# A scan and a bilinear feed-forward network on one core: the hand-written order of all tasks replaced by another, and the zero matmuls in float32

## The chip, the core and the metric

The kernel runs on one core of a Trainium2 chip. The core has a matrix engine (TensorE: PE for its matmuls, PEld for its weight loads), VectorE (DVE), ScalarE (ACT), GpSimd (POOL) and SyncE (SP, which here issues nearly all DMAs). Each engine works off its own list of instructions in order and waits on semaphores for the others. The metric is the device time of one execution in microseconds (us); lower is better.

## What is computed

The inputs are x (4 batches, 8 heads, 768 steps, 32 wide), decays a, and B and C (16 wide). A state per head is carried through time, and its output goes into a feed-forward network with four weight matrices that arrive in float64:

```python
for c in range(nc):                       # pieces of the sequence
    L = np.exp(cum[:, :, :, None] - cum[:, :, None, :]) * causal
    M = np.einsum('bhin,bhjn->bhij', Cc, Bc) * L
    y[:, :, sl] = M @ xc + (Cc @ state) * np.exp(cum)[..., None]
    state = decay_full * state + (Bc * decay_from_j).T @ xc
...
x = y.transpose(0, 2, 1, 3).reshape(3072, 256)
return ((x @ w1) * (x @ w2) @ w3) @ w_out
```

## The kernel before, in words

Every piece of work is a named task, and the string `PLAN` lists all of them in one order. A word `name:engine@banks` says which task comes next, on which engine (V is DVE, S is ACT, G is POOL, nothing is PE or a DMA on SP) and which PSUM banks or slots it gets. The loop at the end walks through the words and records each task; `tc.keep_in_program_order` keeps that order on every engine. So the list alone sets what stands behind what.

The sequence is cut into 16 chunks of 48 steps. For chunk c:
- `cN.X`, `cN.B`, `cN.N` load its inputs (tiles xe, bc, bn), `cN.K` loads decay sums for c of 2 and more. For chunks 0 and 1, `Y0`, `Y1` (DVE) build what `D0`, `D1` (PE) multiply instead; `a.clip`, `a.ln`, `a.scan`, `a.hi`, `a.lo`, `a.save` make the sums that later chunks load as `K`.
- `D0`, `D1` put exponents into a bank, `E0`, `E1` (ACT) take the exponential into tile r, `W0`, `W1` scale B into r, `CB` (PE, four banks) makes C times B, and `M0`, `M1` (DVE) multiply the halves into r.
- `MX` (PE, two banks) multiplies r with xe. `T` (DVE) transposes the state out, eight `Z` copies carry it into the next chunk's xe, and `hi`, `lo` (or `y`) bring the output into xa and xb, split in two float32r parts.

A product in the network is three float32r matmuls (high times high, high times low, low times high). Weights come in as float64 words: `.D` loads one into staging (tile early), then `.A` (ACT), `.L`, `.S` (DVE), `.H`, `.P` make the high and low parts. `wN` are the columns of w1 and w2, `oN` those of w_out, `vHK` those of w3; `vHK.M` (PE) multiplies w3 with w_out, and `e..` moves that into wo.

The 3072 rows are cut into seven slices. For slices 0 to 2, `lS.F.m` (PE) makes the two products, `.a` (ACT) copies one out of PSUM, `.g` (DVE) multiplies it with the other, `.h` and `.l` split the result. Slices 3 and 4, and 5 and 6, go in pairs through `pP.J` (sums of inputs), `zJ` (sums of weights) and seven products `sP.F.1` to `.7`, with `p`, `q`, `r`, `y`, `d`, `g`, `k` between. `dS.F` (PE) multiplies with wo, `dS.yT` copies out and `dS.xT` stores.

A word such as `+8@7` stands for eight matmuls of zeros into bank 7: their result is not used. There are 18, of bfloat16, 512 columns wide (helper `mm`, L151; memset L244). Their tile `zero` is 128 x 512 bfloat16.

The `ring` helper deals out staging slots (four), magnitude slots (five) and slots for w3 (four) in turn. `W` is always on GpSimd (`bw`), `hi` on ACT (`high`) and `.a` on ACT.

Of the kernel before, what the change touches and what calls it, by code (L numbers as in the profile page):

```python
# [30 lines left out]
c1.lo:V w2.S:V w1.A:S w1.L:V w2.H:S w2.P:V c2.D1@2 j.c:S c2.E0:S c1.Z5:S w1.S:V w7.L:V l0.0.m@3,4 w7.A:S w1.H:S w7.S:V l0.2.m@5,0 w1.P:V l0.2.a:S
w6.D w6.A:S c1.Z3:S w7.H:S c1.Z0:S l0.1.m@1,6 w6.L:V l0.2.g:V c3.N w6.S:V w7.P:V w4.D l0.0.a:S c2.B c2.N l0.7.m@7,5 w4.A:S l0.1.a:S c1.Z2:G c2.E1:S
w3.D c3.K c3.B w6.H:V w4.L:V c2.CB@0,1,2,3 w6.P:G l0.0.g:V c1.Z1:G c1.Z6:G c2.W1:G c2.W0:G l0.7.a:S c1.Z4:S w4.S:V l0.1.g:V w5.D c3.X l0.7.g:V
c2.M1:V c2.M0:V w4.H:S w3.A:S c4.B o0.D l0.6.m@4,7 c1.Z7:S w4.P:G w3.L:V w3.S:V w3.H:V w5.L:V c2.MX@5,6 c3.D1@3 c3.D0@2 c2.T:V c3.E1:S c2.hi:S
# [789 lines left out]
```

## Time and profile before

| | us |
|---|---|
| median of 3 runs | 264.28 (263.45 to 265.96) |
| the profiled execution | 263.44 |
| its span, first to last instruction | 261.6 |
| PE busy in it | 254.0 |
| DVE busy in it | 196.8 |

The span is what the trace covers; 1.84 us of the profiled execution's own time lies around it. Busy time is the union of an engine's instructions. Matmuls overlap and their ends are modelled, so a busy PE may still wait inside: the starts of successive matmuls tell more than the busy share. The granted clock of TensorE stands in a row as a share of 2.4 GHz.

### The profile page before, as it was taken

The numbers are of one execution on the slowest core, as the hardware profiler recorded it, in microseconds if no ns is written. First come the engines' busy times: TensorE is split into PE (matmuls) and PEld (weight loads), VectorE is DVE, ScalarE is ACT, GpSimd is POOL, SyncE is SP. The second block draws the span as 40 slices with busy tenths as digits, with TensorE's granted clock in tenths as the row PEclk, the third lists the DMA queues.
The fourth block names the chain that finished last, engine by engine and source line by source line (L and its number), as shares of the span: only waits on it lengthen the run. The fifth ranks groups of instructions, "written<-read, shape, count | busy, mean of one in ns | idle before, by whom it ended". The sixth has DMA issues, their size and how long they took to land.

```text
span 261.6 us, 7416 instructions
## 1 busy us (share of the span) xinstructions
PE 254.0 (97%) x2972; PEld 226.2 (86%) x2972; DVE 196.8 (75%) x354; ACT 141.4 (54%) x308; POOL 121.3 (46%) x160
## 2 busy tenths in 40 slices
...
GB/s 195 323 298 306 231 296 215 279 256 205 272 249 303 247 11 49 196 102 49 147 60 206 65 95 63 83 50 44 4 3 0 0 83 1 0 3 80 3 0 120
DMA packets 21754, 33.93 MB, mean 130 GB/s; under 512 B 3672, under 2 KB 13528, under 8 KB 21720
## 3 DMA queue, kind: packets, MB, share of 16 engines
...
HBM read 30.02 MB, written 3.44 MB: 128 GB/s over the span
## 4 chain that ended last, share of the span: by engine, by line
PE 85%; DMA 5%; DVE 4%; ACT 3%; issue 1%; SPq 0%; DVEq 0%
PE ps L151 85%; DMA xe<-in_x_dram 2%; DMA bc<-in_c_dram 2%; ACT fr L163 1%; DVE gs L157 1%; DMA gs<-in_Bt_dram 1%; DVE early L480 1%; DVE fr L157 0%; DVE early L160 0%; SPq L154 0%; ACT g L163 0%; ACT r L166 0%; DVE z L402 0%; ACT early L166 0%; ACT wo L163 0%
## 5 line engine op out<-in xcount | busy, mean ns | idle before, releaser
L151 PE MATMUL ps<-wo,fr 128*128 128x256 f32 x576 | 71.4, 281 | 0.0
L151 PEld LDWEIGHTS ps<-wo,fr 128*128 128x128 f32 x576 | 69.4, 189 | 1.2
L157 DVE TENSOR_TENSOR gs<-gs,ps 128x512 f32<-128x512 f32 (+1 forms) x73 | 43.6, 623 | 15.9 <-PE ps L151 10.4
L151 PE MATMUL ps<-xa,wh 128*128 128x384 f32 (+1 forms) x192 | 54.9, 366 | 0.2 <-DVE xa L157 0.2
L163 ACT COPY gs<-ps 128x512 f32<-128x512 f32 (+2 forms) x53 | 25.3, 492 | 47.6 <-PE ps L151 41.9
L151 PEld LDWEIGHTS ps<-xa,wh 128*128 128x128 f32 x192 | 34.6, 188 | 4.1 <-DVE xa L157 0.4
L151 PE MATMUL ps<-op,tw 128*128 128x512 f32 (+1 forms) x144 | 35.1, 366 | 0.0
L151 PE MATMUL ps<-xa,wl 128*128 128x384 f32 (+1 forms) x96 | 34.9, 363 | 0.0
L157 POOL TENSOR_TENSOR r<-bn,r 128x128 f32<-128x128 f32 x32 | 16.0, 507 | 35.5 <-ACT xe L163 13.6
L151 PEld LDWEIGHTS ps<-op,tw 128*128 128x128 f32 x144 | 25.8, 188 | 3.1 <-DVE gs L157 0.3
L157 POOL TENSOR_TENSOR fr<-gs,fr 128x512 fp32r<-128x512 f32 (+1 forms) x21 | 25.6, 1227 | 6.0 <-DVE fr L163 2.9
L151 PE MATMUL ps<-fr 128*128 128x256 f32 x192 | 25.4, 286 | 0.2 <-DVE fr L157 0.2
L151 PEld LDWEIGHTS ps<-fr 128*128 128x128 f32 x192 | 24.0, 191 | 1.2 <-DVE fr L157 0.4
L163 POOL COPY xe<-z 16x128 f32<-16x128 f32 x40 | 15.8, 394 | 14.4 <-issue 5.1
L157 DVE TENSOR_TENSOR r<-ps,r 128x384 f32<-128x384 f32 x32 | 17.2, 550 | 5.6 <-PE ps L151 4.8
L163 ACT COPY xe<-z 16x128 f32<-16x128 f32 x65 | 19.2, 296 | 1.6 <-DMA xe<-in_x_dram 0.3
L151 PEld LDWEIGHTS ps<-xa,wl 128*128 128x128 f32 x96 | 18.0, 188 | 2.0
L163 POOL CAST fr<-gs 128x384 fp32r<-128x384 f32 (+1 forms) x10 | 6.0, 601 | 28.5 <-PE ps L151 20.1
L166 ACT ACTIVATE early<-early 128x512 f32<-128x512 f32 x23 | 15.5, 675 | 6.1 <-DMA early<-in_w3t_dram 2.8
L480 DVE SCALAR_TENSOR_TENSOR early<-early 128x512 uint32<-128x512 uint32 x23 | 17.5, 760 | 1.4 <-ACT early L166 0.8
L163 ACT CAST fr<-gs 128x512 fp32r<-128x512 f32 (+1 forms) x23 | 13.8, 602 | 8.5 <-PE ps L151 8.4
L151 PE MATMUL ps<-op,wh 128*128 128x512 f32 (+1 forms) x64 | 18.2, 365 | 0.0
...
## 6 DMA issues: line engine op xcount, KB each, us to landing
...
bc<-in_Ct_dram SPq DMA_DIRECT2D x14, 320.0 KB, 4.6
xe<-in_x_dram SPq DMA_DIRECT2D x16, 256.0 KB, 4.1
early<-in_w_dram SPq DMA_DIRECT2D x16, 256.0 KB, 4.6
...
out_dram<-gs SPq DMA_DIRECT2D x22, 128.0 KB, 2.1
...
bn<-in_Bn_dram SPq DMA_DIRECT2D x14, 128.0 KB, 3.1
```

What stands on the lines that cost most here:

```text
L151: pin(nc.tensor.matmul(*args, **kw))
L157: pin((nc.gpsimd if e == "G" else nc.vector).tensor_tensor(*args))
L163: pin(nc.scalar.copy(*args) if e == "S" else (nc.gpsimd if e == "G" else nc.vector).tensor_copy(*args))
L166: pin(nc.scalar.activation(*args, **kw))
L480: pin(nc.vector.scalar_tensor_tensor(m, m, 3, v["wl"].bitcast(U32), ALU.logical_shift_left, ALU.bitwise_or))
```

## The change

The list of tasks is another one from the first word to the last: the tasks are the same (but for the zeros), with another order, other engines for 227 of them, and other banks and slots. Words in the list now also choose the staging and magnitude slot, the slot for w3, and the engine of `W`, `hi` and `.a`, so `ring` is gone. The matmuls of zeros are 6 (four at the start, two before `c1.MX`), and their operand is the first 512 columns of the tile fr, read as float32.

```diff
 PLAN = """
-t.D k.zero:V k.act:S +8@7 k.D1:D a.D c0.X t.clip:V c0.B c0.N w0.D t.ln:S k.R0:S k.keep:G k.L:V c0.Y0:V +1@7 c0.D0@0 a.clip:V a.ln:S c1.X k.D2:D c1.N
+k.zero:V k.act:S k.keep:G t.D k.D1 a.D w2.D@0 c1.N c0.N w0.D@1 a.clip:V c0.B t.clip:V k.L:V t.ln:S c0.X k.R0:S c1.Y0:V k.D2 c0.Y1:V a.ln:S +4@2
...
-    zero = sb([P, 512], BF16, "zero")
+    zero = FR[:, 0:512].bitcast(F32)
...
-        def bw(hf):
+        def bw(e, hf):
             gs = slice(hf * HG, (hf + 1) * HG)
-            tt("G", R[:, gs, 0:N], bp[:, gs, :], R[:, gs, TE - 1:TE].broadcast_to([P, HG, N]), ALU.mult)
+            tt(e, R[:, gs, 0:N], bp[:, gs, :], R[:, gs, TE - 1:TE].broadcast_to([P, HG, N]), ALU.mult)
...
-        def high(*at):
-            copy("S", place(0, *at), py(*at[1:]))
+        def high(e, *at):
+            copy(e, place(0, *at), py(*at[1:]))
...
-            v["st"] = ST[ring("st", NST)]
+            v["st"] = ST[b[0]]
...
-            v["mag"] = MAG[ring("mag", NMAG)]
+            v["mag"] = MAG[b[0]]
...
-            v["hi"], v["lo"] = hi(), lo()
+            v["hi"], v["lo"] = hi(b), lo()
...
-            slot["t"] = VR[:, ring("vr", 4)]
+            slot["t"] = VR[:, b[0]]
...
-            gate[sl, ft] = G5[k // 3][:, k % 3] if k < 15 else FREE[8][:, :384] if k == 15 else FREE[ft]
-            copy("S", gate[sl, ft], v[0])
+            gate[sl, ft] = G5[k // 3][:, k % 3] if k < 15 else FREE[b[0]][:, :BL[sl]]
+            copy(e, gate[sl, ft], v[0])
```

What the list does is seen in the instructions of each engine. On SP, the first eleven loads of before are these (la, gs and the array a are for the decays; early is staging for w0; xe, bc, bn belong to chunks 0 and 1 by their number):

```order
L154 DMA la<-in_Bt_dram 128x256
L154 DMA gs<-in_Bt_dram 128x352
L154 DMA gs<-in_a_dram 128x192
L154 DMA xe_82<-in_x_dram 128x512
L154 DMA bc_87<-in_c_dram 128x640
L154 DMA bn_84<-in_b_dram 128x256
L154 DMA early<-in_w_dram 128x2x256 x2
L154 DMA xe_83<-in_x_dram 128x512
L154 DMA gs<-in_Bt_dram 128x144
L154 DMA mask<-in_Bt_dram 128x48
L154 DMA bn_85<-in_b_dram 128x256
```

and of the change, where tile numbers are one lower from ld on:

```order
L154 DMA la<-in_Bt_dram 128x256
L154 DMA gs<-in_Bt_dram 128x352
L154 DMA gs<-in_a_dram 128x192
L154 DMA early<-in_w_dram 128x2x256 x2
L154 DMA bn_84<-in_b_dram 128x256
L154 DMA bn_83<-in_b_dram 128x256
L154 DMA early<-in_w_dram 128x2x256 x2
L154 DMA bc_86<-in_c_dram 128x640
L154 DMA xe_81<-in_x_dram 128x512
L154 DMA gs<-in_Bt_dram 128x144
L154 DMA mask<-in_Bt_dram 128x48
L154 DMA bc_87<-in_c_dram 128x640
```

Two whole weight loads, w2 and w0, now stand ahead of chunk 0's bc and xe, and chunk 1's bc and xe follow at once.

On PE, these are the last zeros ahead of `c0.D1` of before and then the tasks `c0.D1`, `c0.CB`, `c1.D0`, `c0.MX`, `c1.D1`, `c1.CB` (rd and gs are the two matmuls of a `D`, bc is `CB`, r with xe is `MX`):

```order
L151 MATMUL ps<-zero 128x512
L151 MATMUL ps<-rd,ld 128x384
L151 MATMUL ps<-gs 128x384
L151 MATMUL ps<-bc_87 64x96 x16
L151 MATMUL ps<-rd,ld 128x384
L151 MATMUL ps<-gs 128x384
L151 MATMUL ps<-r_89,xe_82 32x64 x32
L151 MATMUL ps<-rd,ld 128x384
L151 MATMUL ps<-gs 128x384
L151 MATMUL ps<-bc_88 64x96 x16
```

and the first rows of the change, where fr stands for the zeros and the tasks are `c1.D0`, `c0.D1`, `c0.D0`, `c0.CB`, `c1.D1`, `c0.MX`, `c1.CB`:

```order
L151 MATMUL ps<-fr 128x512 x4
L151 MATMUL ps<-rd,ld 128x384
L151 MATMUL ps<-gs 128x384
L151 MATMUL ps<-rd,ld 128x384
L151 MATMUL ps<-gs 128x384
L151 MATMUL ps<-rd,ld 128x384
L151 MATMUL ps<-gs 128x384
L151 MATMUL ps<-bc_86 64x96 x16
L151 MATMUL ps<-rd,ld 128x384
L151 MATMUL ps<-gs 128x384
L151 MATMUL ps<-r_88,xe_81 32x64 x32
L151 MATMUL ps<-bc_87 64x96 x16
```

Three `D` tasks now stand in a row ahead of `c0.CB`, and none is left between `c0.MX` and `c1.CB`.

On DVE, behind chunk 3's first `M` (r1 from ps) before, up to `c3.lo` (xb from ps), which frees chunk 3's banks:

```order
L157 TENSOR_TENSOR r1_90<-ps_66,r1_90 128x8x48
L480 SCALAR_TENSOR_TENSOR early_94<-early_94 128x512
L157 TENSOR_TENSOR r1_90<-ps_66,r1_90 128x8x48
L163 CAST wh_96<-early_94 128x512
L157 TENSOR_TENSOR wl_97<-early_94,wh_96 128x512
L402 STREAM_TRANSPOSE z_91<-ps_66 128x256
L157 TENSOR_TENSOR g1_69<-g1_69,ps_66 128x384 x2
L160 TENSOR_SCALAR early_94<-early_94 128x512
L157 TENSOR_TENSOR xb_93<-ps_66,xb_93 128x2x192
```

and of the change, from the first `M` of chunk 3 to the same `c3.lo`:

```order
L157 TENSOR_TENSOR r1_89<-ps_66,r1_89 128x8x48
L157 TENSOR_TENSOR g1_69<-g1_69,ps_66 128x384
L157 TENSOR_TENSOR r1_89<-ps_66,r1_89 128x8x48
L160 TENSOR_SCALAR early_93<-early_93 128x512 x2
L157 TENSOR_TENSOR wl_96<-early_93,wh_95 128x512
L474 SCALAR_TENSOR_TENSOR early_93<-early_93 128x512 x2
L160 TENSOR_SCALAR early_93<-early_93 128x512
L396 STREAM_TRANSPOSE z_90<-ps_66 128x256
L157 TENSOR_TENSOR xb_92<-ps_66,xb_92 128x2x192
```

Between the second `M` of chunk 3 and `c3.lo`, before has w5's cast and low part, the transpose, two `.g` and one `.L`; the change has w5's low part, the transpose and five steps of the weights v10, v11, o0 and v13. In the change `c4.CB`, second on PE behind `c3.MX`, writes banks 2 and 3, which `c3.lo` reads; before it takes the same banks, with `l0.5.m` and `l1.5.m` ahead of it.

## Rows read from the trace of the kernel before

**Rows 1.** The head of the page: the span, and each engine's busy time, share of the span and instructions.

```profile
span 261.6 us, 7416 instructions
...
PE 254.0 (97%) x2972; PEld 226.2 (86%) x2972; DVE 196.8 (75%) x354; ACT 141.4 (54%) x308; POOL 121.3 (46%) x160
```

**Rows 2.** The timeline of PE and its weight loads: start us, length us, engine, line, operation, tiles, shapes, count, and in brackets idle time ahead and what ended it. The first nine rows are of the start up to 17.22 us and the tenth is where the stream of `l0.0.m` begins for good; the last two are where `l0.5.m` starts and where it is followed by `l1.5.m`.

```profile
1.19 3.73 PE L151 MATMUL ps<-zero 128*128 128x512 bf16 x9 [1.19 <-DVE zero L244]
...
1.59 0.15 PEld L151 LDWEIGHTS <-zero 128*128 128x128 bf16 x1 [0.28 <-issue]
...
2.02 0.15 PEld L151 LDWEIGHTS <-zero 128*128 128x128 bf16 x1 [0.28 <-issue]
...
4.84 0.44 PE L151 MATMUL ps<-rd,ld 48*128 48x384 f32 x1
...
5.21 0.91 PE L151 MATMUL ps<-gs 128*128 128x384 f32 x2
...
5.96 0.81 PE L151 MATMUL ps<-zero 128*128 128x512 bf16 x3
...
7.92 0.59 PE L151 MATMUL ps<-bc 32*64 32x96 f32 x32
...
9.64 0.89 PE L151 MATMUL ps<-r,xe 64*32 64x64 f32 x64
...
12.06 0.59 PE L151 MATMUL ps<-bc 32*64 32x96 f32 x32 [0.31 <-DMA bc<-in_c_dram]
...
17.22 0.45 PE L151 MATMUL ps<-xa,wh 128*128 128x384 f32 x1 [0.15 <-DVE xa L157]
...
36.20 0.52 PE L151 MATMUL ps<-xa,wh 128*128 128x384 f32 x2
...
38.32 0.51 PE L151 MATMUL ps<-xb,wh 128*128 128x384 f32 x2
```

**Rows 3.** Three stretches: busy time of PE, PEld, DVE, ACT and POOL with their instructions, then granted clock, DMA share, GB/s.

```profile
0.00:6.00 6.00, 4.82 (x13) 1.81 (x14) 2.43 (x8) 3.25 (x5) 0.57 (x6) 1.00 0.64 187
6.00:10.00 4.00, 4.00 (x77) 1.88 (x76) 2.59 (x7) 1.88 (x4) 0.82 (x2) 1.00 1.03 332
17.20:38.40 21.20, 21.06 (x292) 19.52 (x293) 18.80 (x37) 15.72 (x36) 8.57 (x15) 1.00 0.85 284
```

**Rows 4.** DMA issues: tiles, engine, count, KB each, and where it is known the median us from issue to landing.

```profile
la<-in_Bt_dram SPq DMA_DIRECT2D x1, 128.0 KB
...
gs<-in_Bt_dram SPq DMA_DIRECT2D x1, 176.0 KB
...
gs<-in_a_dram SPq DMA_DIRECT2D x1, 96.0 KB
...
early<-in_w_dram SPq DMA_DIRECT2D x16, 256.0 KB, 4.6
...
bn<-in_b_dram SPq DMA_DIRECT2D x2, 128.0 KB, 4.4
...
bc<-in_c_dram SPq DMA_DIRECT2D x2, 320.0 KB, 4.5
...
xe<-in_x_dram SPq DMA_DIRECT2D x16, 256.0 KB, 4.1
```

**Rows 5.** The timeline of the start on DVE, POOL and ACT (columns as in rows 2): the memset of zeros, the first `W`, chunk 0's `M0` and `M1`, `c1.hi`, `c1.lo`.

```profile
0.86 0.27 DVE L244 MEMSET zero<- 128x256 uint32 x1 [0.86 <-PEq L805]
...
7.57 0.41 POOL L157 TENSOR_TENSOR r<-bn,r 128x128 f32<-128x128 f32 x1 [6.42 <-DMA bn<-in_b_dram]
...
8.61 1.02 DVE L157 TENSOR_TENSOR r<-ps,r 128x384 f32<-128x384 f32 x2 [1.40 <-PE ps L151]
...
16.09 0.48 ACT L163 CAST xa<-ps 128x384 fp32r<-128x384 f32 x1 [1.70 <-DVE z L402]
...
16.61 0.56 DVE L157 TENSOR_TENSOR xa<-ps,xa 128x384 fp32r<-128x384 f32 x1 [0.55 <-ACT xa L163]
```

**Rows 6.** DVE from 17.18 to 38.5 us, groups of one line and shape: count, busy us, mean ns of one, idle us ahead. In order: `.S`, `.g`, `.L`, `.P`, `M`, `T`.

```profile
L480 DVE SCALAR_TENSOR_TENSOR early<-early 128x512 uint32<-128x512 uint32 x7 | 5.5, 781 | 0.2
L157 DVE TENSOR_TENSOR g<-g,ps 128x384 f32<-128x384 f32 x7 | 3.6, 540 | 0.0
L160 DVE TENSOR_SCALAR early<-early 128x512 uint32<-128x512 uint32 x7 | 3.5, 495 | 0.0
L157 DVE TENSOR_TENSOR wl<-early,wh 128x512 fp32r<-128x512 f32 x4 | 2.8, 689 | 0.4 <-ACT wh L163 0.3
L157 DVE TENSOR_TENSOR r<-ps,r 128x384 f32<-128x384 f32 x4 | 2.1, 553 | 0.7 <-POOL r L157 0.6
L402 DVE STREAM_TRANSPOSE z<-ps 128x256 f32<-128x256 f32 x2 | 0.9, 446 | 0.5 <-PE ps L151 0.5
```

**Rows 7.** The timeline of PE's weight loads at three waits: ahead of `c5.MX`, in `v02.M`, ahead of `c8.MX`.

```profile
56.59 0.19 PEld L151 LDWEIGHTS ps<-r,xe 64*32 64x32 f32 x10 [0.64 <-ACT fr L163]
...
79.18 1.25 PEld L151 LDWEIGHTS ps<-fr 128*128 128x128 f32 x10 [0.45 <-DVE fr L157]
...
105.44 0.72 PEld L151 LDWEIGHTS ps<-r,xe 64*32 64x32 f32 x64 [0.93 <-ACT fr L163]
```

**Rows 8.** The timeline of DVE: one `z0.B`, which runs while POOL works.

```profile
97.65 2.33 DVE L157 TENSOR_TENSOR gs<-wh,wl 128x1024 f32<-128x1024 f32 x1
```

**Rows 9.** The group of all three `zJ.B` on DVE over the whole span: count, busy us, mean ns.

```profile
L157 DVE TENSOR_TENSOR gs<-wh,wl 128x1024 f32<-128x1024 f32 x3 | 4.9, 1631 | 0.0
```

More of the change, by code (lines that the diff above doesn't have):

```diff
@@ L31 @@
[L31 to L34, printed above, removed]
@@ new lines @@
+o0.H:S v10.P:G c3.T:V v12.D@3 c4.E1:S c3.lo:V v00.D@1 l0.3.g:V c4.CB@0,1,2,3 l0.5.a:S c4.W0:G c4.W1:V v11.A:S@4 l1.7.m@6,7 c4.M0:V c9.F1:G c7.N
+v13.A:S@2 c4.M1:V c5.B v11.S:V c6.N c3.Z1:G c3.Z3:V c8.K c9.F0:G c5.D1@0 l0.5.g:V c5.D0@1 l1.7.a:S@8 l1.5.m@2,3 c5.E0:S v12.L:V c3.Z4:G c5.X c3.Z0:S
+c3.Z6:G c6.B c3.Z5:S o1.D@0 v00.L:V c6.K l1.1.m@4,1 v13.S:V l1.5.a:S v11.H:S@1 l1.5.g:V c9.G1:V c3.Z7:S v02.D@2 v00.A:S@0 v11.P:G l1.4.m@6,5
+l1.1.a:S c3.Z2:S l1.1.g:V c5.W0:G c5.E1:S o0.P:V c5.W1:G l1.7.g:V c8.F1:G c4.MX@0,1 l1.4.a:S v12.A:S@3 l1.4.g:V c5.CB@6,7,3,4 c8.F0:G c4.hi:S c4.T:V
```

144 lines of the change are left out of this document (70 added, 74 removed).

## Prediction

> **What bounds the kernel now.** I read the page first: PE is busy for 254.0 of 261.6 us [rows 1], so the change can give only what PE still waits, and what lies ahead of its dense stream and behind it. Then the timeline of PE [rows 2]: what matters is when successive tasks start. Until 17.22 us the small products of chunks 0 and 1 and the zeros run; from 17.22, when `c1.lo` has ended, PE hardly stops. Then the stretches [rows 3]: DMA moves 332 GB/s from 6 to 10 us, so early on it is loads that are waited for; and from 17.2 to 38.4 DVE is busy for 18.80 of 21.20 us, so it is nearly a second bound there. Last the places where PE's weight loads stood still in the stream [rows 7]: 0.64, 0.45 and 0.93 us. A better order can win about these, and no more.
>
> The sum is made against the profiled execution, 263.44 us. The median of the three runs stands 0.84 us above it.
>
> **The zeros.** Before, weight loads of zeros start 0.43 us apart (1.59, 2.02) [rows 2]: 512 columns in 0.43 us are 1.2 GHz, the lower level. Three zeros at 5.96 take 0.81 us together, which is more columns in a us than the lower level has, so the clock is up by then. The nearest row for float32 is the second matmul of a `D`: 384 columns as two passes, from 5.21 to 5.96, so 0.75 us; 512 columns take 1.0 us at that clock, and at half of it 2.0 us as an upper end. The memset [rows 5] is twice as large, so the first zero starts not at 1.19 but about 0.27 later, at 1.46. If the clock is up by 4.84, as before, 3.4 us hold 1.7 zeros, and the other 2.3 end at 7.15. Three `D` follow, 1.12 us each (4.84 to 5.96): 10.5. If all four zeros run at the lower level they end at 9.5, and the `D` tasks at 12.8.
>
> **The loads.** How long a load takes is checked with chunk 0's bn: with it 1,104 KB have been issued (la 128, gs 176, a 96, xe 256, bc 320, bn 128 [rows 4]), or 1,130 kB. 187 GB/s move 1,122 kB by 6 us [rows 3], so its last byte moves at 6.0, and POOL, which waits for it, starts at 7.57 [rows 5]: 1.5 us more. In the change, chunk 0's bc is the last of 2,000 KB (la, gs, a, two halves of w2, two bn, two halves of w0, bc): 2,048 kB move by 8.8 us at 332 GB/s, and it lands at 10.3. Its xe is 256 KB later, at 11.1, and chunk 1's bc, 576 KB later, at 12.1. So `c0.CB` starts at about 10.5 instead of 7.92. The zeros and three `D` just fill the time until the load is there.
>
> **From there to the stream.** Before, `c0.CB` at 7.92 was followed by both `M` (8.61, 1.02 us [rows 5]) and `c0.MX` at 9.64 [rows 2], 1.72 us on. So `c0.MX` starts at 12.2 now and `c1.CB` 0.8 us behind it, at 13.0; before it started at 12.06, when its load was there. `CB` takes 0.5 us, the two zeros 2.0 us: 15.5. The `T` and both `M` that `c1.MX` needs end at about 15.2, so the zeros cost 0.3 us. `c1.MX` 0.8 us, a handover of 0.1, `c1.hi` 0.48 and `c1.lo` 0.56 [rows 5] (`c1.T` now stands behind them, which saves 0.45) give 17.5. **Start: +0.3 us**; at the fast end, with zeros that hide and loads 0.5 us earlier, -0.4; with all zeros at the lower level +2.3.
>
> **c2.D0 and c2.D1** stood ahead of 17.22, in PE's wait. Now they stand behind `l0.0.m`, because `a.lo` and so `a.save` come later on DVE and SP. A float32r product of 384 columns takes 0.18 us in `l0.5.m` (twelve from 36.20 to 38.32) and 0.37 us as the first matmul of a `D` (4.84 to 5.21) [rows 2], so two take 0.36 to 0.74; I take **+0.4**, near the former, since later loads overlap.
>
> **DVE in the first stretch.** From 17.22 to 38.32 PE does eight `l0` products, two `CB`, two `MX`, four `D` [rows 2]: 21.1 us. In the change the same work and two more `D`, 21.5 us, lies between the end of `c1.lo` and `c4.CB`, which must wait for `c3.lo` to free its banks. In the same stretch DVE's list has 41 instructions: 8 `.S` at 0.781, 9 `.L` at 0.495, 5 `.P` at 0.689, 6 `.g` and a copy like it at 0.540, 4 `M` at 0.553, 3 `T` at 0.446 [rows 6], two `lo` at 0.56 [rows 5], and three small ones, taken as 0.3 each. That is 6.25 + 4.46 + 3.45 + 3.78 + 2.21 + 1.34 + 1.12 + 0.9 = 23.5 us, where before had 18.80 in 21.2 us. DVE has done less ahead of 17.22 and takes on the first w3 and w_out weights earlier. So `c4.CB` could be 2.0 us late. Some of the 0.781 is stretch from other engines: a `.P`, also with two inputs and 512 columns, takes 0.689, and with that `.S` would save 0.7. I take **+1.3**; 0 if DVE finds that much slack, 3.0 with 1 us of waits for ACT's casts. Behind it are `l1.7.m`, which waits for `l0.3.g` just behind `c3.lo`, and the rest of PE's list.
>
> What a busy POOL does to DVE is seen in one pair of rows [rows 8, 9]: one `z0.B` took 2.33 us, while the three have 1.631 as mean, so the other two 1.28; a factor of 1.8. The change gives POOL `.H` of w7, w4, w3 and w5 and two `.P` in this stretch. The Trainium skill, GPSIMD Engine Reference, Specifications, says that GpSimd shares its SBUF interfaces with VectorE and contends with DVE instructions that have two SBUF inputs (or run in a two-port mode). By that rule `.S` and `.P` are all open to it, and the sum would come to the slower rival's 267.6. The rows' means speak for little of it, and I follow the means.
>
> **The waits that go.** Ahead of `c5.MX` (0.64) PE waited for a carry that stood behind `c5.M0` on DVE; in the new list chunk 4's carries come before that `MX` with `l1.2.g` between. In `v02.M` (0.45) it waited for `v02.P`, which stood right ahead of it in the list and now stands five PE tasks earlier. **-1.0** for both, 0 at worst. The third (0.93) stays: `c9.CB` and `c8.MX` share two banks and stand next to each other in both lists.
>
> **Sum:** 263.44 + 0.3 + 0.4 + 1.3 - 1.0 = 264.4. The rest is costed at nothing: the products are the same, and behind the last matmul there are three copies on the same two engines and three stores, as before.
>
> **Rivals.**
> - Faster. DVE keeps up (+0) as it starts the weights' steps in PE's small waits, the start is even or 0.4 early, and all waits go, the third among them (-2.0): 263.44 - 0.4 + 0.4 - 2.0 = 261.4, and with one half of that 262.4. For it: before, DVE had 2.4 us free in the same stretch. Against it: the sum of 23.5.
> - Slower, by POOL alone (the rule above): the 13 `.S` and `.P` of the stretch, 9.7 us, are stretched by POOL's casts. By a third each is +3.2 on top of 1.3: 267.6. Decides from 2.5 us of stretch (266.9). For it: the stretched row [rows 8]. Against it: the `.S` of before ran beside 8.57 us of POOL work [rows 3] and took 0.781 all the same.
> - The zeros don't save anything, but hold PE: all four at the lower level, start +2.3: 266.4. Against it: the clock was up by 5.96 before, and PE runs as densely now.
>
> **How the numbers follow.** My sum has 0.45 (263.2 to 265.6), the faster case 0.29 (261.0 to 263.2), the slower one 0.18 (266 to 268), the zeros 0.08. The range of 8 in 10 leaves out the end of the faster case and that of the slower: 261.3 to 267.3. About 1% is what a measurement of this kernel can tell from no change; around the median of before that is 261.6 and 266.9. Below lies half of the faster case, with noise 0.17; above lie three quarters of the slower one, and some of the zeros: 0.18; within is 0.65.
>
> **What would show it.** Right: `c0.CB` at 10 to 11 us waiting for bc or just behind the `D`; the second matmul of `l0.0.m` at 17.2 to 17.9; PE waiting 1 to 2 us for DVE at `c4.CB` or `l1.7.m`; no wait in `v02.M`, and one of 0.9 us at `c8.MX`. Wrong: a stream that starts before 16.7 or after 18.5; `.S` above 0.95 us in the first stretch; no wait of PE around 38 to 40 us; or new waits of over 1 us in the stretch of the `sP.F` products, which I have not costed as DVE has more room there.

## The result, and the profile after

| | before | change |
|---|---|---|
| median, four runs each | 264.78 us (263.45 to 265.96) | 267.43 us (266.59 to 268.16) |
| ratio, 95% interval | | 1.0118 (1.0078 to 1.0158) |
| the profiled execution | 263.44 | 267.43 |
| start of the second matmul of `l0.0.m` | 17.22 | 18.42 |
| start of `v10.M` | 58.17 | 61.37 |
| start of the last PE task, `d6.7` | 256.25 | 260.48 |

The change is slower by 1.2%. Two later sets of six runs of it gave 1.0126 (1.0083 to 1.0169) and 1.0145 (1.0106 to 1.0183). The last rows cut the time in three. Between the second matmul of `l0.0.m` and `v10.M` both lists do the same PE work, but for `c2.D0` and `c2.D1`, which are 0.35 us: 40.96 us before and 42.94 now. From `v10.M` to `d6.7` the work is the same too: 198.08 and 199.12. So the start lost 1.2 us, the middle 2.0, the rest 1.0. This cut is of one profiled execution of each: that of before is the fastest of its four, that of the change lies at its median, so they differ by 4.0 us where the medians differ by 2.65.

The page of the change, span and busy times [rows 1]:

```profile
span 265.6 us, 7397 instructions
...
PE 257.4 (97%) x2966; PEld 227.0 (85%) x2966; DVE 203.1 (76%) x362; ACT 133.5 (50%) x288; POOL 131.4 (49%) x172
```

PE is busier by 3.4 us with the same products: its zeros take 8.3 us (6.33 and 1.98 below) where those of before took 6.0, which is 2.3 of it, and a matmul that waits inside counts as busy. The start of PE's timeline [rows 2] tells more (fr are the zeros):

```profile
1.45 6.33 PE L151 MATMUL ps<-fr 128*128 128x512 f32 x8 [1.45 <-DVE fr L238]
7.71 0.44 PE L151 MATMUL ps<-rd,ld 48*128 48x384 f32 x1
...
8.92 0.44 PE L151 MATMUL ps<-rd,ld 48*128 48x384 f32 x1
...
11.34 0.59 PE L151 MATMUL ps<-bc 32*64 32x96 f32 x32
...
13.19 0.86 PE L151 MATMUL ps<-r,xe 64*32 64x64 f32 x64
13.97 0.59 PE L151 MATMUL ps<-bc 32*64 32x96 f32 x32
14.49 1.98 PE L151 MATMUL ps<-fr 128*128 128x512 f32 x4
16.40 0.86 PE L151 MATMUL ps<-r,xe 64*32 64x64 f32 x64
...
17.83 1.03 PE L151 MATMUL ps<-xa,wh 128*128 128x384 f32 x2
19.02 0.33 PE L151 MATMUL ps<-xa,wl 128*128 128x384 f32 x1 [0.16 <-issue]
```

And the weight loads of the zeros, in PEld's timeline:

```profile
5.03 0.34 PEld L151 LDWEIGHTS ps<-fr 128*128 128x128 f32 x1 [0.52 <-issue]
5.88 0.34 PEld L151 LDWEIGHTS ps<-fr 128*128 128x128 f32 x1 [0.52 <-issue]
6.74 0.22 PEld L151 LDWEIGHTS ps<-fr 128*128 128x128 f32 x1 [0.52 <-issue]
...
15.03 0.19 PEld L151 LDWEIGHTS ps<-fr 128*128 128x128 f32 x1 [0.24 <-issue]
15.45 0.19 PEld L151 LDWEIGHTS ps<-fr 128*128 128x128 f32 x1 [0.24 <-issue]
```

A zero is recorded as two matmuls of 512 columns (x8 for the four), and one of these takes 0.85 us until 6.74 and 0.42 us at 15: of the first four zeros three ran at the lower level (1.45 to 6.74), and the fourth took 0.97 us. The three `D` tasks are 1.21 us apart, not 1.12.

The places in the stream where PE stood [rows 7], in its timeline:

```profile
40.37 0.59 PE L151 MATMUL ps<-bc 32*64 32x96 f32 x32 [0.33 <-DMA bc<-in_Ct_dram]
...
43.67 0.58 PE L151 MATMUL ps<-rd,ld 96*128 96x384 f32 x2 [0.42 <-DMA ld<-cq]
...
108.15 0.86 PE L151 MATMUL ps<-r,xe 64*32 64x64 f32 x64 [0.72 <-DVE r L157]
...
185.21 1.65 PE L151 MATMUL ps<-op,tw 128*128 128x512 f32 x6 [0.53 <-DVE gs L163]
```

These are `c4.CB`, `c5.D1`, `c8.MX` and `s0.6.7`. By the starts, against the usual distance of such tasks, they are 0.60, 0.67, 0.79 and 0.69 us late. (The usual distance is taken as 2.11 us from one `l` product to the next; ahead of a `CB` or a `D` it is 2.2 to 2.3 where nothing waits, so such a figure can be 0.2 too large. A wait inside a `MX` shows as lateness of the task behind it.) The third was there before; the others are new. The stretches of [rows 3], and with them the one from the second matmul of `l0.0.m` to `c4.CB`:

```profile
0.00:6.00 6.00, 4.55 (x6) 1.97 (x7) 2.25 (x7) 2.69 (x4) 0.56 (x6) 1.00 0.60 179
6.00:10.00 4.00, 4.00 (x10) 1.40 (x8) 2.70 (x7) 1.66 (x4) 1.27 (x2) 1.00 0.98 311
17.20:38.40 21.20, 20.89 (x293) 18.74 (x289) 19.53 (x40) 14.09 (x31) 9.13 (x17) 1.00 0.86 278
18.42:40.37 21.95, 21.46 (x293) 19.59 (x294) 20.41 (x42) 14.94 (x33) 10.46 (x19) 1.00 0.86 276
```

### The profile page after: what moved, and what is told of

It is laid out like the page before. It is cut to its first block, busy times and chain, and to the rows that moved or that the text cites. A ratio compares the mean times of both kernels' runs of the same rounds, so it can differ in the third digit from the quotient of the medians.

```text
span 265.6 us, 7397 instructions
## 1 busy us (share of the span) xinstructions
PE 257.4 (97%) x2966; PEld 227.0 (85%) x2966; DVE 203.1 (76%) x362; ACT 133.5 (50%) x288; POOL 131.4 (49%) x172
## 4 chain that ended last, share of the span: by engine, by line
PE 73%; DMA 13%; DVE 7%; SPq 3%; issue 2%; DVEq 0%; ACT 0%; ACTq 0%
PE ps L151 73%; DMA early<-in_w_dram 6%; SPq L154 3%; DMA early<-in_w3t_dram 2%; DVE gs L157 2%; DMA ct<-cd 2%; DMA cd<-gs 2%; DMA bc<-in_Ct_dram 1%; DVE r L157 1%; DVE early L474 1%; DVE g L157 1%; DVE gs L163 0%; DVE early L160 0%; DVE xe L163 0%; DVE z L396 0%
## 5 line engine op out<-in xcount | busy, mean ns | idle before, releaser
L163 ACT COPY gs<-ps 128x512 f32<-128x512 f32 (+2 forms) x46 | 22.3, 496 | 40.2 <-PE ps L151 26.7
L157 POOL TENSOR_TENSOR fr<-gs,fr 128x384 fp32r<-128x384 f32 (+1 forms) x20 | 23.6, 1192 | 34.6 <-DVE fr L163 26.9
L151 PE MATMUL ps<-fr 128*128 128x256 f32 (+1 forms) x204 | 33.2, 318 | 1.6 <-DVE fr L238 1.5
L151 PEld LDWEIGHTS ps<-fr 128*128 128x128 f32 x204 | 26.9, 196 | 6.2 <-issue 3.6
L163 POOL COPY xe<-z 16x128 f32<-16x128 f32 x47 | 19.4, 413 | 10.8 <-DVE z L396 7.3
L157 POOL TENSOR_TENSOR r<-bn,r 128x128 f32<-128x128 f32 x25 | 14.9, 604 | 9.4 <-ACT r L166 6.0
L163 ACT COPY xe<-z 16x128 f32<-16x128 f32 x56 | 16.6, 296 | 3.9 <-DVE z L396 2.2
L163 DVE COPY gs<-ps 128x256 f32<-128x256 f32 (+2 forms) x19 | 9.3, 505 | 10.1 <-PE ps L151 9.9
L151 PE MATMUL ps<-xb,wh 128*128 128x384 f32 x64 | 16.6, 340 | 0.0
L474 DVE SCALAR_TENSOR_TENSOR early<-early 128x512 uint32<-128x512 uint32 x21 | 16.5, 798 | 0.1
```

The source lines that it names most:

```text
L151: pin(nc.tensor.matmul(*args, **kw))
L157: pin((nc.gpsimd if e == "G" else nc.vector).tensor_tensor(*args))
L163: pin(nc.scalar.copy(*args) if e == "S" else (nc.gpsimd if e == "G" else nc.vector).tensor_copy(*args))
L474: pin(nc.vector.scalar_tensor_tensor(m, m, 3, v["wl"].bitcast(U32), ALU.logical_shift_left, ALU.bitwise_or))
```

## The experiments

Starts and waits that stand here without a row are from the timeline and the waits of the run named; "late" is by the starts, against the usual distance of such tasks.

### What the zeros do

**e1**, the change with bfloat16 zeros:

```diff
-    zero = FR[:, 0:512].bitcast(F32)
+    zero = FR[:, 0:256].bitcast(BF16)
-... a.ln:S +4@2 c1.D0@0 ... w2.P:V +2@5 c1.MX@2,3 ...
+... a.ln:S +9@2 c1.D0@0 ... w2.P:V +6@5 c1.MX@2,3 ...
```

> The change with the zeros of before: nine of bfloat16 at the start, six ahead of c1.MX, order otherwise that of the change. Theory 'zeros': in the change the four float32 zeros end at 7.71 us and hold the D tasks, so here zeros end near 5.2, c0.CB starts when chunk 0's bc is there, 10.3 to 10.7 instead of 11.34, and the second matmul of l0.0.m at 17.3 to 17.7 instead of 18.42; time about 266.5 where the change took 267.43. Theory 'loads': c0.CB is set by the landing of bc alone, stays at 11.2 to 11.4, and the stream starts at 18.2 or later; time 267.4.

269.25 us, 1.0205 (1.0147 to 1.0263). `c1.D0` started at 5.62 instead of 7.71, and then PE waited 1.48 us for chunk 0's bc. What followed is in the stretches (the column behind the five engines is the granted clock):

```profile
9.30:10.80 1.50, 0.02 (x1) 0.00 (x0) 0.79 (x3) 0.82 (x2) 0.18 (x1) 1.00 1.07 383
10.80:11.80 1.00, 0.99 (x33) 0.76 (x33) 0.60 (x1) 0.99 (x3) 0.67 (x2) 0.99 0.98 363
11.80:15.20 3.40, 3.40 (x91) 1.90 (x98) 1.33 (x3) 1.57 (x3) 1.92 (x3) 0.50 0.90 279
```

Then PE waited 1.83 us in `l0.0.m` for a weight that DVE made, and the second matmul came at 20.60:

```profile
20.35 0.58 PE L150 MATMUL ps<-xa,wh 128*128 128x384 f32 x2 [1.83 <-DVE early L473]
```

Neither theory held. bc came at 10.8, so without the zeros `c0.CB` starts 0.53 us earlier and no more: here bc is its floor. The stretch of half clock followed the wait. How much of the late stream is the clock's and how much DVE's is not shown. From the second matmul to `v10.M` this run took 41.87 us.

**e5**, the change with one zero fewer:

```diff
-... a.ln:S +4@2 c1.D0@0 ...
+... a.ln:S +3@2 c1.D0@0 ...
```

> The change with three float32 zeros ahead of the first decay matmul instead of four; nothing else differs. Theory A (the start is late because each float32 zero takes 1.7 us at the lower clock level): the zeros end near 6.0 instead of 7.7, c1.D0 starts there, and PE then runs until it meets bc, which landed at 10.8 in the run with bfloat16 zeros: c0.CB near 10.8 instead of 11.3, the second matmul of l0.0.m near 17.8 instead of 18.4, the time 0.5 us under the change, near 266.9. Theory B (the fourth zero is what keeps the clock up until bc lands): PE waits over 0.5 us for bc, a stretch of half granted clock follows, second matmul of l0.0.m after 19.5, the time 268.5 or more. Theory C (the start is set by ACT's and DVE's chain to c1.lo and not by PE): l0.0.m where it was, 267.4.

268.84 us, 1.0171 (1.0117 to 1.0225). PE waited 0.90 us for bc, the clock was 0.50 from 12 to 15 us, and the second matmul of `l0.0.m` came at 19.13. So theory B has the wait and the half clock right, but the stream came 0.7 us later and not after 19.5. The time can't be put on the zero: its interval overlaps the change's, and in this profile PE also waited 2.9 us for bc ahead of `c4.CB`.

**e2**, the kernel before with six float32 zeros:

```diff
-    zero = sb([P, 512], BF16, "zero")
+    zero = FR[:, 0:512].bitcast(F32)
-... k.act:S +8@7 ... +1@7 ... +3@7 ... +6@7 ...
+... k.act:S +4@7 ... +2@7 ...
```

> Before with four float32 zeros for its first nine (and for the three behind c0.D0, which go), and two for the six ahead of c1.MX; order otherwise that of before. Theory 'zeros': they end at 7.2 to 7.8 instead of 4.84, the D tasks run behind them, c1.CB moves from 12.06 to 13.5 to 14.5 and the second matmul of l0.0.m from 17.22 to 18.5 to 19.2; time 1.3 to 2 us over before. Theory 'loads': the loads of chunk 1 are waited for anyway, so the stream starts at most 0.4 us later and the time is that of before.

264.8 us, 1.001 (0.9977 to 1.0043). In its profile the second matmul of `l0.0.m` is at 18.57, 1.35 us later than before, from there to `v10.M` it takes 40.59 us (40.96 before), and `d6.7` starts 1.3 us later. The medians show no more than 0.4% of it. A late start by itself does not make the change's 1.2%.

**e8**, before's start ahead of the change's rest. Its banks of `c2.D0` and `j.m` are written again by `l0.1.m` and `l0.2.m` before they are read, so chunk 2's exponents and the running sums are not the reference's:

```diff
-k.zero:V k.act:S k.keep:G t.D ... (the change's words up to c1.lo)
+t.D k.zero:V k.act:S +8@7 k.D1 a.D c0.X ... c1.lo:V (before's words, with slots)
-... +2@5 c1.MX@2,3 c2.X w4.D@3 w1.L:V ... w1.S:V ...
+... w1.L:V ... w1.S:V w4.D@3 ...
```

> The whole of before's start, up to c1.lo, with its bfloat16 zeros (18 of them) and its order on all engines, ahead of the change's order for the rest; w4.D stands behind w1.S, since w1 sits in its staging slot until then. Theory (a term of the sum was too small: the start costs 1.2 to 1.5 us more than before's, forecast 0.3): second matmul of l0.0.m near 17.2, and 1.2 to 1.5 us come off the change, near 266.0. Rival (DVE decides from there to c4.CB, so that an earlier start of PE is given back): second matmul of l0.0.m near 17.2, but the wait ahead of c4.CB and c5.D1 grows from 1.27 to 2 us or more, and the time is within 0.5 us of 267.4. Rival 2 (this start doesn't fit this rest, as w2, w1 and w7 are converted later in it): new waits in l0.1.m to l0.7.m, the time over 268.5.

269.5 us, 1.0201 (1.0161 to 1.0242). The start did not come out as meant: the second matmul of `l0.0.m` was at 18.38, as PE waited 0.9 us for `c1.lo` (xa), and then 1.2 us for a weight and 2.1 us for ld. Rival 2; the run says nothing on the start's worth. A first form of it, e3, had `w4.D` ahead of w1's steps, into the staging slot that w1 still sat in, and the same two banks too early. Its theory was a second matmul at 17.2 to 17.5 and 266.0 us; it came at 18.11, PE waited 2.1 us for a cast of weights and 1.4 for a low part, the clock was 0.50 from 27.3 to 30.8, and it took 273.76 us, 1.0362 (1.0291 to 1.0433). It says nothing on the start either.

### Loads, and the change again

**e4**, loads moved on SP:

```diff
-... c4.K ... v11.D@0 ... c4.N ... v13.D@2 ... c4.B ... c9.K ... c5.K ... c8.K ... c6.K ...
+... c4.K c4.B ... v11.D@0 ... c4.N ... v13.D@2 ... c5.K c9.K ... c6.K c8.K ...
```

> The change with three words moved: c4.B right behind c4.K, c9.K behind c5.K, c8.K behind c6.K, so that SP no longer holds chunk 4's and chunk 5's loads behind the wait for chunk 9's. Theory 'SP order': PE's waits ahead of c4.CB (0.60 us over the usual spacing) and c5.D1 (0.67) go, and the time falls by 0.8 to 1.3 us to about 266.3. The prediction's theory 'DVE sum': c4.CB waits for c3.lo and l1.7.m for l0.3.g on DVE, so the waits stay within 0.3 us and the time is 267.2 or more.

269.53 us, 1.0225 (1.0172 to 1.0277). The wait for bc went, but PE now waited 1.1 us for `c3.lo` (xb) and 0.5 for `l0.3.g`, and 0.4 for an exponent of chunk 3 too: the loads that had been pushed back held DVE, 2.2 us for w3t and 0.8 for bn.

**e7**, DVE and loads eased around `c4.CB`:

```diff
-... v13.D@2 ... c4.B ... c9.K ... c5.K ... c8.K ... c6.K ...
+... c4.B v13.D@2 ... c5.K c9.K ... c6.K c8.K ...
-... w5.H:G ... v10.L:V ... v11.L:V ... w5.P:V ... v13.L:V ... c3.lo:V ... l0.3.g:V ...
+... w5.H:G ... v10.L:V ... w5.P:V ... c3.lo:V ... l0.3.g:V v11.L:V v13.L:V ...
```

> The change with v11.L and v13.L moved behind l0.3.g on DVE (1.0 us of work that nobody waits for yet), c4.B issued just ahead of v13.D, and c9.K and c8.K issued behind c5.K and c6.K. Theory (c4.CB and c5.D1 wait because DVE's list up to c3.lo and l0.3.g is longer than PE's, and because the loads behind it are late): neither end is late any more, the 0.60 us ahead of c4.CB and the 0.67 us ahead of c5.D1 fall under 0.2 us each, and the time is 1.0 us under the change, near 266.4. Rival (DVE's sum over the stretch decides, so work that is moved behind l0.3.g delays the next thing, c4.M0, c4.M1 or l0.5.g): c4.CB starts earlier but as much waiting stands at l1.7.m, l1.5.m or c4.MX, and the time is within 0.4 us of 267.4. Rival 2 (the loads alone decided): the releaser named ahead of both is gone and nothing is left to wait for, again near 266.4, but c3.lo ends over 0.5 us ahead of c4.CB.

269.3 us, 1.0198 (1.0154 to 1.0241). `c4.CB` and `c5.D1` did not wait, and yet nothing was won: `c3.D1` waited 1.0 us, and `l1.3.m` started 1.4 late, with 0.74 of it a wait inside `c5.MX` for a carry that POOL copies (xe).

**e12, e16**, the change itself, twice more (no edit):

> The change itself, unaltered, on the chip of the three others, as what they are read against and as a second profile of it. Theory (the loads come just in time, so an execution with a longer hold of SP waits longer): c4.B is issued somewhere between 35.7 and 37.6, the wait ahead of c4.CB lies between 0.6 and 3 us and follows that time, and the times spread from 266.5 to 269.5. Rival (the 3 us of two other runs came from their own edits): 0.6 us ahead of c4.CB again and times of 266.6 to 268.2.

> The change itself on the chip of the other three, to read them against. 266.6 to 268.6, with waits from c2.D1 to v10.M that sum to 2 to 5 us and fall on other places than in its first two profiles, if late loads with varying landing times cause them; the same places with the same sizes, if DVE's order does.

267.94 and 268.31 us. In e12's profile PE's waits from 17 to 64 us are

```profile
PE ps L151 <- DMA bc<-in_Ct_dram: 1.3, 1, 1.3
PE ps L151 <- issue: 0.8, 1, 0.8
```

and in e16's

```profile
PE ps L151 <- DVE g L157: 1.9, 1, 1.9
PE ps L151 <- ACT r L166: 0.8, 1, 0.8
PE ps L151 <- DMA ld<-cq: 0.5, 1, 0.5
```

The same list waits at other places each time. By the starts, `c4.CB` was 0.60 us late in the first profile, 1.59 in e12, 0.24 in e16. e6, further below, has the change's order up to `s0.6.r`, and there it was 2.98:

```profile
PE ps L150 <- DMA bc<-in_Ct_dram: 2.7, 1, 2.7
PE ps L150 <- DMA ld<-cq: 0.5, 1, 0.5
```

From the second matmul of `l0.0.m` to `v10.M` these four took 42.94, 43.47, 45.26 and 46.16 us. In the order first profile, e12, e16, e6, c4's bc was issued at 35.73, 36.91, 36.19 and 36.57 us, and `c4.CB` stood 4.6, 5.1, 4.6 and 6.7 us behind it: the time of the issue alone doesn't set how late it gets. DVE waits for loads as well. In all, it waited 1.6, 2.1, 2.2 and 2.4 us for w3t (the weights w3 in staging) from 18 to 63 us, and never in before. In e12 its `.L` of v13, ahead of `c3.lo`, waited 1.54:

```profile
40.73 0.64 DVE L160 TENSOR_SCALAR early<-early 128x512 uint32<-128x512 uint32 x1 [1.54 <-DMA early<-in_w3t_dram]
...
41.66 0.51 DVE L157 TENSOR_TENSOR xb<-ps,xb 128x384 fp32r<-128x384 f32 x1
```

The second row is `c3.lo`. It ended at 42.17, behind the start of `c4.CB` at 42.01, so there DVE was as late as bc, whatever the profile names. In e16 the 1.9 us ahead of `v10.M` are a wait for `l1.3.g`, and in front of that DVE waited 0.85 us for w3t and then took 1.49 for an `.L` that usually takes 0.42, beside a `.P` on POOL:

```profile
60.88 1.49 DVE L160 TENSOR_SCALAR early<-early 128x512 uint32<-128x512 uint32 x1 [0.85 <-DMA early<-in_w3t_dram]
...
60.82 1.26 POOL L157 TENSOR_TENSOR fr<-early,fr 128x512 fp32r<-128x512 f32 x1
```

**e9**, the four stores of the running sum, which stand ahead of c4's loads, moved behind them:

```diff
-... a.keep ... c4.N ... v13.D@2 ... c4.B ... c9.K ... c5.K ... v00.D@1 ... c8.K ... c6.K ...
+... c4.N ... v13.D@2 ... c4.B ... c5.K ... v00.D@1 a.keep ... c6.K c9.K c8.K ...
-... c9.F1:G ... c9.F0:G ... c9.G1:V ... c8.F1:G ... c8.F0:G ...
+... c6.W0:G c9.F1:G c9.F0:G c8.F1:G c8.F0:G ... l1.3.g:V c9.G1:V ...
```

> The change with the four stores a.keep (cd<-gs) moved on SP's queue from ahead of c4.N, v13.D and c4.B to behind v00.D, the two loads that read them (c9.K, c8.K) to behind c6.K, and the five steps on POOL and DVE that use those behind c6.W0 and l1.3.g. Theory (the stores hold SP for 2.6 to 3.7 us right ahead of the loads that c4.CB and c5.D1 need, and how long they hold it differs between executions): c4.B is issued near 32.5 instead of 35.7 to 37.6, the wait ahead of c4.CB is under 0.3 us where the change has 0.60 in one execution and 2.98 in another with the same order, c5.D1 doesn't wait, no stretch around 43 to 47 has half the granted clock, and the time is 1.3 to 2.5 us under the change, near 265.5. Rival (DVE's sum: c3.lo and l0.3.g are as late as before, whatever the loads do): c4.CB waits 0.3 to 0.6 us and l1.7.m about 0.5 us more, the time within 0.6 us of 267.4.

271.81 us, 1.028 (1.0236 to 1.0323). The stores (cd) and c4's bc in SP's timeline of the change

```profile
31.37 2.61 SPq L154 DMA_DIRECT2D cd<-gs  x4
...
35.73 0.38 SPq L154 DMA_DIRECT2D bc<-in_Ct_dram  x1
```

and of e6, where SP was held longer:

```profile
31.78 3.74 SPq L153 DMA_DIRECT2D cd<-gs  x4
...
36.57 0.67 SPq L153 DMA_DIRECT2D bc<-in_Ct_dram  x1
```

In e9 bc was issued at 33.70, and neither `c4.CB` nor `c5.D1` waited. That part of the theory holds; the time went the other way, with 2.1 us at `l1.3.m`, 1.7 at `c6.CB` and 0.9 at `v11.M`, where PE waited for DVE's products and for POOL. Ahead of `l1.2.g`, the product that was late for `l1.3.m`, DVE had itself waited 1.35 us for w3t. POOL was held by the steps that use the stored words. Another 2.2 us went at the start of the stream, where PE stood for 1.17 us and half clock followed (last section); no execution of e9 took under 270.42 us, though in two of them the granted clock was 0.999 or 1.000 on the mean.

**e10** (the running sum saved early) and **e11** (both):

```diff
-... w2.A:S@0 c0.Y0:V w2.L:V c1.X a.scan:V ... c1.E0:S w2.S:V a.hi:S ... a.lo:V ... a.save ...
+... a.scan:V a.hi:S w2.A:S@0 c0.Y0:V a.lo:V w2.L:V c1.X ... a.save c1.E0:S w2.S:V ...
```

> The change with the running sum's chain as early as its inputs allow: a.scan and a.hi ahead of w2.A, a.lo ahead of w2.L, a.save ahead of c1.E0. In the change a.hi stands behind c1.E0 on ACT, so behind the first matmul of c1.D0 on PE, a.save is issued at 10.5 (7.2 before), and w1, w7, w6 and c2.K stand behind it on SP's queue. Theory D (SP's 2.3 us of waiting there puts the weights late, and with them everything to c4.CB): a.save near 7.9, w1.D near 8.5 instead of 10.9, c2.K near 11.5 instead of 14.0, and the time 0.5 to 1.5 us under the change, near 266.4. Rival (the transfers are queued deep enough that an earlier issue changes nothing, or DVE's conversions bind): the same issue times, but c4.CB and c5.D1 wait as in the change, the time within 0.4 us of 267.4.

> Both edits together: the stores behind the loads that are needed first, and the running sum saved early. If both theories hold and their gains add: 264.6 to 265.5, about the kernel before. If only the stores matter: as that run, near 265.5. If neither does: 267.4.

e10: 269.08 us, 1.0168 (1.0127 to 1.0209); a.save was issued at 8.75 and the stream began at 17.79, but `c4.CB` and `c5.D1` were 0.86 and 0.95 us late, and `v10.M` 2.16. e11: 270.36 us, 1.0219 (1.017 to 1.0268). It took only 41.87 us to `v10.M`, as e1 did, the shortest of all lists with this rest, and reached it earliest, at 59.66, with no wait at `c4.CB` or `c5.D1`, and lost 3 us behind it: 202.16 us from `v10.M` to `d6.7` instead of 199.12, first at `v11.M`, with POOL the releaser (xe, 1.6 us).

**e13, e14**, the loads first, POOL's steps where it has room, `s0.6.r` on ACT; with and without the early sum. The stores and loads are moved as in e9, and in e13 the sum as in e10; what comes on top of that is shown:

```diff
-... c9.F1:G ... c9.F0:G ... c9.G1:V ... c8.F1:G ... c8.F0:G ... c8.G1:G ... c8.G0:V ...
+... c4.Z1:G c9.F1:G c9.F0:G ... l1.3.g:V c9.G1:V ... c6.Z6:G c8.F1:G c8.F0:G c8.G1:G ... l1.6.g:V c8.G0:V ...
-... s0.6.3 c15.E1:S s0.6.r:V@4 ...
+... s0.6.3 c15.E1:S s0.6.r:S@4 ...
```

> The change with the running sum saved early, the four stores a.keep behind v00.D, c9.K and c8.K behind c6.K, the two steps of c9 on POOL behind c4.Z1 and those of c8 behind c6.Z6, and s0.6.r on ACT. Theory (late loads and this one copy are what the change loses after its start): no wait over 0.3 us from c2.CB to v11.M, c6.CB near 58.2 (60.6 in the change), none at s0.6.7, the time 2.5 to 3 us under the change's in this call, near 264.7. Rival (every order of this rest finds another wait, since DVE and the transfers are both nearly full there): 1 us or more of new waits at v10.M to v11.M or later, the time within 1 us of the change's.

> As the one before, but with the running sum saved as late as the change saves it. Theory: a.save at 10.5 and the weights behind it cost what they cost in the change (start and c2.D1 about 0.6 to 1 us later than with the early sum), the rest as there: near 265.5. Rival (the early sum is worth nothing by itself, as its own run without the stores' move showed 269): the same time as the one before, within 0.4.

269.4 us, 1.0183 (1.0138 to 1.0228), and 268.6 us, 1.0168 (1.0126 to 1.021). In both `c4.CB`, `c5.D1` and `s0.6.7` had no wait over 0.2 us, and to `v10.M` it took 43.26 and 42.97 us all the same. In e13:

```profile
PE ps L150 <- DVE g L156: 1.7, 2, 1.5
PE ps L150 <- issue: 0.5, 1, 0.5
```

The rival holds: the wait had moved to `l1.3.m` (1.74 and 1.94 us late), for DVE's products. What held DVE there was in e13 once more a load, 1.46 us for w3t right ahead of `l1.2.g`; in e14 an `.L` at 55.77 took 1.49 us beside a `.P` on POOL.

**e15**, the same loads made late in the kernel before:

```diff
-... c4.B o0.D ... w5.P:V v13.D ... a.keep c5.B ...
+... o0.D ... w5.P:V a.keep v13.D c4.B ... c5.B ...
```

> The kernel before with a.keep ahead of v13.D and c4.B behind it, which is the order that the change has at this place: c4.B is issued near 36.5 instead of 26.3, c4.CB on PE stands at 40.5. Theory (such a late load is what PE waits for): c4.CB waits 0.3 to 2 us for bc, and the time is 0.5 to 2 us over the kernel before. Rival (a transfer that is issued 4 us ahead is in time, or the wait is absorbed later): no wait over 0.2 us at c4.CB, the time within 0.4 us of the kernel before.

263.75 us, 1.0001 (0.9972 to 1.003). The load was issued at 34.54 instead of 26.29, and PE did wait for it:

```profile
PE ps L150 <- DMA bc<-in_Ct_dram: 0.6, 1, 0.6
```

But to `v10.M` it took 40.71 us, and the total is that of before: the theory is right on the wait and the rival on the time. Why, its profile shows: the wait that before had at `c5.MX` is not there. In before, DVE had waited for a stored sum ahead of a carry that this `MX` needs:

```profile
54.43 0.56 DVE L157 TENSOR_TENSOR ct<-ct,la 128x384 f32<-128x384 f32 x1 [1.52 <-DMA ct<-cd]
```

e15 and e2, with the same order of carries as before, have neither that wait of DVE nor the one at `c5.MX`. So that wait hung on how a load landed in one execution, and not on the order of the carries.

### DVE's order, and the copy in the sP.F products

**e17** moved conversions on DVE behind what PE waits for; **e18** is that with the loads of e14 and `s0.6.r` on ACT:

```diff
-... v13.L:V ... c4.M1:V ... v12.L:V v00.L:V ... c9.G1:V l1.1.g:V ... l1.7.g:V l1.4.g:V ...
+... c4.M1:V v13.L:V ... l1.1.g:V v12.L:V ... l1.7.g:V c9.G1:V l1.4.g:V v00.L:V ...
-... v00.S:V ... l1.2.a:S ... v02.L:V ... l1.2.g:V ... v04.L:V ... l1.3.g:V ...
+... l1.2.a:S l1.2.g:V v00.S:V ... l1.3.g:V v02.L:V v04.L:V ...
```

> The change with, on DVE, v13.L behind c4.M1, v12.L behind l1.1.g, v00.L behind l1.4.g, v02.L and v04.L behind l1.3.g, c9.G1 behind l1.7.g, and l1.2.g (with ACT's l1.2.a) ahead of v00.S; no load is moved. Theory H (DVE's list is held at steps that wait for loads which nobody on PE needs yet): DVE's waits for w3t ahead of l1.3.g fall from about 2 us to under 0.7, the waits at l1.3.m and v10.M (0.8 to 2 us together in the change's three profiles) to under 0.4, and the time 1 to 1.5 us under the change's 267.4 to 268.3, near 266.6. Rival (DVE's sum of work or the transfers' rate bind): the waits move to v11.M or v00.M, which need the delayed conversions, or stand at c4.CB and c5.D1 for bc and ld, and the time is within 0.5 us of 268.

> The same on DVE, with the four stores behind v00.D, c9.K and c8.K behind c6.K, c9's two steps on POOL behind c4.Z1, c8's behind c6.Z6, and s0.6.r on ACT. If late loads and a held DVE together make the loss after the start: waits from c2.CB to v11.M under 1 us in all, c6.CB near 58.6, s0.6.7 without its wait, the time near 265. If only one of them: near 266.5. If DVE's own sum or the transfers bind: 268 again, with new waits after v10.M.

271.34 us, 1.0256 (1.0216 to 1.0296), and 269.31 us, 1.0218 (1.0172 to 1.0263). DVE's waits for w3t are gone, and in their place stand waits for ACT's `.a` copies; e17's first rows for DVE from 18 to 63 us:

```profile
DVE g L156 <- ACT g L162: 2.3, 2, 1.6
DVE g L156 <- PE ps L150: 1.9, 2, 1.5
```

PE lost it up to `l1.3.m` (1.77 us, 1.1 of it inside `c5.MX`, for a carry on DVE that now stands behind `l1.2.g`) and at `v00.M` (1.87), and `c4.CB` waited 1.0 for bc all the same: the rival. Theory H falls. Part of it is of my making, since `l1.2.g` came too early in DVE's list, ahead of its copy on ACT and of that carry.

**e6**, the change with one copy back on ACT:

```diff
-... s0.6.3 c15.E1:S s0.6.r:V@4 ...
+... s0.6.3 c15.E1:S s0.6.r:S@4 ...
```

> The change with the one copy s0.6.r on ACT, as the kernel before has it, instead of DVE. Theory (the 0.69 us that PE waits ahead of s0.6.7 comes from this copy's place in DVE's queue): that wait is under 0.2 us and the time 0.5 to 0.7 us under the change, near 266.8. Rival (ACT is late there too, or the next step of the sP.F stretch waits in its place): the waits from s0.6.1 to c14.MX sum to what they did, 267.4.

267.97 us, 1.0144 (1.0102 to 1.0187): by the time nothing can be told, since the interval covers the change's; the profiled execution (269.39) was 2.4 us later at `c4.CB` than the change's first, and half clock followed from 43.4 to 46.8. By the profile the theory holds: `s0.6.7` does not wait in e6, e13, e14 and e18, and is 0.67 to 0.74 us late in the change's three profiles and e4, e7, e9 and e10, and 1.0 and 0.9 in e11 and e17. From `v10.M` to `d6.7` e6 takes 198.32 us, the change 198.61 to 199.16, before 198.08.

## Why the prediction was off, step by step

The forecast was 264.4 us, 1.0 over the profiled execution of before; the change's median is 267.43. Sorted by the three stretches of the result, its terms and what the change's three profiles show over before are:

| us over before | forecast | first profile | e12 | e16 |
|---|---|---|---|---|
| start | +0.3 | +1.20 | +1.24 | +0.40 |
| middle | +1.1 (0.4 + 1.3 - 0.64) | +1.98 | +2.51 | +4.30 |
| rest | -0.4 | +1.04 | +0.53 | +1.08 |

Two steps failed. The start was put too low for two of the three profiles, by 0.9 us. And from there on the sum booked 1.0 us of waits as won by the new order and nothing for waits behind `c4.CB`, where the runs show 2.0 to 4.3 us lost up to `v10.M` and 0.5 to 1.1 behind it. The second step weighs more: e16's start was the forecast's (17.62 against 17.5), and its profile is the slowest of the three, 269.0 us; e2's start was 1.35 us late, and its median is within 0.2% of before's.

- **The start: a term that was mis-sized** (+0.3; +1.2 in the first profile). The zeros were put at 1.7 at the lower level and 2.3 at the upper; in the profile three ran at the lower, as the clock came up at about 6.7 and not 4.84. They ended at 7.71 (forecast 7.15) and the `D` tasks took 1.21 us each (forecast 1.12), so `c0.CB` stands at 11.34 (10.5). From there the chain fits: 1.85 us to `c0.MX` (forecast 1.7), 0.8 to `c1.CB`, 1.9 for the zeros, 2.0 from `c1.MX` to the second matmul of `l0.0.m`. In ten profiles of lists with this head that matmul lies between 17.62 and 18.46, +0.4 to +1.2. A zero at the lower level is 1.70 us, not the 2.0 of the upper end. The load's landing, forecast at 10.3, was 10.8 in e1 and 10.5 in e5. What I had as a rival (zeros that hold PE) was a matter of degree: in e16, where the clock came up first, the start is +0.4.
- **c2.D0 and c2.D1** (+0.4): 0.34 us, from 20.78 to 21.12. Right.
- **c4.CB and what follows** (+1.3): 1.27 us in the first profile, 0.60 and 0.67, but by another mechanism, so that the size agrees is luck. The profile names bc and ld, and `c3.lo`, in this row of DVE, had ended at 39.99, 0.38 us ahead of `c4.CB` and about where that would have started without a wait:

```profile
39.47 0.52 DVE L157 TENSOR_TENSOR xb<-ps,xb 128x384 fp32r<-128x384 f32 x1
```

  In e12 DVE was late too, but by a load it waited for, and not by its sum. Loads put ahead took the waits away in four lists whose `c3.lo` was as it was (e9, e11, e13, e14). DVE's sum of 23.5 us was too much: its instructions overlap, as in these two rows of the change's DVE, the first 0.52 us long, the second 0.44 behind it:

```profile
59.70 0.52 DVE L157 TENSOR_TENSOR g<-g,ps 128x384 f32<-128x384 f32 x1
60.14 0.41 DVE L160 TENSOR_SCALAR early<-early 128x512 uint32<-128x512 uint32 x1
```

  From 18.42 to 40.37 DVE was busy for 20.41 us of 21.95, with 42 instructions, and their durations sum to 22.6, so a sum of single durations gives some 2 us too many. I had seen the load's move on SP in the list and not costed it: the four stores ahead of it hold SP for 2.6 to 3.7 us.
- **The waits that go** (-1.0). The one in `v02.M` went. The one at `c5.MX` came back inside the same task in the first profile, where `l1.3.m` is 0.55 us late behind it, and in e16 three tasks on, `v10.M` 1.95. And neither was shown to come from the order that I put it on: e15, in before's order, has neither, and e2 has only `v02.M`'s. I read them in one profile, took them for the list's, and did not ask what DVE's list, now with a later product, would be late with next. The 0.9 us at `c8.MX` stayed, as said.
- **The sP.F products** (0): `s0.6.7` is 0.7 us late, since `s0.6.r` moved from ACT to DVE. I had the move in the list and had left the stretch out because DVE had room on the average.
- **The slower rival, POOL,** falls in the stretch that it was set for. From 18.42 to 40.37 POOL was busy for 10.46 us, and the eight `.S` took 0.71 us each on the mean, before 0.78:

```profile
L474 DVE SCALAR_TENSOR_TENSOR early<-early 128x512 uint32<-128x512 uint32 x6 | 4.2, 722 | 0.1
...
L474 DVE SCALAR_TENSOR_TENSOR mag<-mag,early 128x512 uint32<-128x512 uint32 x2 | 1.4, 689 | 0.3 <-ACT mag L166 0.3
```

  Behind it the matter is open. From 41 to 66 us each DVE instruction that took over 1.4 times (and over 0.25 us more than) the median of its like overlaps one of POOL, as e16's two rows above show, and what they took over that median sums to 2.0, 1.9, 3.7 and 3.0 us in the first profile, e12, e16 and e6, against 0.5 to 0.6 in before, e2 and e15. That is coincidence in time: no run took POOL's work away.

What the middle of the change loses is shown as a sum (1.6 to 4.0 us over before in its three profiles, once the two `D` are taken off) and as places. The copy `s0.6.r` is the one cause that an edit and its return show. How the middle divides between loads that PE waits for, loads that DVE waits for, DVE's own order and POOL beside it stays open: with the loads put ahead PE waits for DVE, with DVE's conversions put back DVE waits for ACT, and no list with the change's rest that I ran beat the change, let alone before.
